# Transformer block: moving the hand-over from the key projection to the row maxima, and the loads around it

## The chip, the cores and the metric

The kernel runs on one core of one Trainium2 chip. The engines that do its work are TensorE (PE, with its weight loads shown apart as PEld), VectorE (DVE), ScalarE (ACT) and GpSimd (POOL). SyncE (SP) only issues transfers to the DMA engines, one after the other; its rows in a profile (SPq) show the issue, not the transfer. The metric is device time in microseconds (us), the median of several runs, lower is better. Before the change it is 1687.12 us, the median of three runs (1686.07 to 1687.93).

## The reference

One block with attention and an MLP, both scaled and shifted by a conditioning vector. S = 2048 positions, D = 512, 32 heads of 16, F = 1792, all in float32:

```python
mod = (_silu(c) @ w_mod).reshape(c.shape[0], 6, 1, -1)
sa, ca, ga, sb, cb, gb = (mod[:, i] for i in range(6))
h = _layernorm(x) * (1 + ca) + sa
qkv = h @ wqkv                                   # q, k, v: 32 heads of 16
p = softmax((q @ k.T) * 16 ** -0.5)              # full, 2048 x 2048 in each head
x = x + ga * ((p @ v) @ wo)
h = _layernorm(x) * (1 + cb) + sb
a = h @ w1 + b1
x = x + gb * ((a * tanh(softplus(a))) @ w2)
```

## The kernel before, in words

**Numbers in two halves.** Most operands of the products are split into a high part that TensorE multiplies in one pass and a low part that holds the rest (`hi_copy`, `lo_sub`, lines 86 to 95: names end in `h` and `l`). A product is then the sum of three: high by high, high by low, low by high (`mm3`).

**Projections (first part, up to about 48 us).** The normalised input is transposed into `h_h` and `h_l`, four blocks of 512 positions (`tb` 0 to 3). The weights of q, k and v come in slices (`slice_load`, tile `wr`), split by `slice_split` (L88 on ACT makes `wh`, L95 on POOL makes `wl`). `qk_unit` multiplies one slice by one block: 128 rows, which are 8 heads. Its `fin` takes the product out of its PSUM bank, splits it (`qh`, `ql`) and stores it in DRAM in `qscr` or `kscr`, each of the 16 rows of a head threefold: 48 rows. `v_unit` does the same for v, collects four blocks of 128 positions in a tile `vq` and stores them in `vscr` (L306). In the first part only slice 0 of the keys (all four blocks), slice 0 of the queries (block 0) and a little of v are made.

**Pairs.** Heads are worked on four at a time (a group, `n`), two and two: pair 0 and 1 are group 0, pair 2 and 3 group 1. `load_pair(pp)` loads a pair's queries (`load_q`, L321, tile `qa`, 50 rows for each head) and keys (`load_k`, L330, tile `ka`, 48 rows of 2048, with two more rows that a memset has filled with ones). For pairs 0 and 1 the keys are loaded block by block. There are five `qa` and five `ka` tiles (`NR`).

**Maxima (steps -20 to -1).** Before a group's scores are taken through the exponential, the maximum of each query's scores must be known. `max_pair` makes the scores of 128 queries against 512 keys for two heads (L596 on PE, into two banks of the `ring` in PSUM) and DVE reduces them to a maximum (L598, `mx`). Thirty-two such products serve group 0, eight more begin group 1. `neg_max` (L611, DVE) ends the reduction of a group, `max_rows` transposes the result (L617 on PE), ACT and DVE split its negative (`mh`, `mt`), and four small DMAs (L626, here called the rows of maxima) put it in rows 48 and 49 of the queries, where the ones in the keys add it to each score. The ring has four banks free for these products, two pairs, so PE can be two products ahead of DVE. Between two products PE does dense work: units of the projections still to do (`dense_slots`, `lanes`; L133).

**Main part (steps 0 to 511).** Each step makes scores (L637), takes their exponential on ACT (L640), multiplies an earlier step's by v (L655, tile `vg`, loaded by `load_v`, L569), makes products for the maxima of the next group (L582, reduced by L584) and, beside it, dense work: projections, then the output projection and the MLP. Weights of the MLP are split and put in DRAM ahead of time; the first six that way during the maxima (`early_load` and `early_prep`, tile `ep`, stored by L1595).

**What sets the order.** It is written out by hand. Each step `t` has two hook numbers, `h` = 2t and 2t + 1, and `at(h, f)` puts the work `f` at such a point. Nothing reorders it: each engine, and SP's queue, runs its instructions in that order, and each instruction waits for its own operands and buffers. A hook number therefore is a place in the order of each engine and no time. The maxima stage begins at `h` = -40, the scores at 0.

Of the kernel before, what the change touches and what calls it, by code (L numbers as in the profile page):

```python
# [8 lines left out]
F32 = mybir.dt.float32  # L9
# [9 lines left out]
def adaln_block(ctx: ExitStack, tc: tile.TileContext, x, wqkv, wo, w1, b1, w2, c, w_mod, out):  # L19
    nc = tc.nc  # L20
# [8 lines left out]
    NB = S // TB  # L29
# [53 lines left out]
    def dap(t, off, ap):  # L83
        return bass.AP(tensor=t.tensor, offset=t.offset + off, ap=ap)

    def hi_copy(eng, hi, src):
        if eng == "a":
            nc.scalar.copy(hi, src)  # L88
        elif eng == "v":
            nc.vector.tensor_copy(hi, src)  # L90
        else:
            nc.gpsimd.tensor_scalar(hi, src, 1.0, 0.0, op0=ALU.mult, op1=ALU.add)

    def lo_sub(eng, lo, src, hi):
        (nc.gpsimd if eng == "p" else nc.vector).tensor_sub(lo, src, hi.bitcast(F32))  # L95
# [15 lines left out]
    def mm3(acc, ah, al, bh, bl, late="a"):  # L111

        n = len(ah)
        seq = ((ah, bh), (ah, bl), (al, bh)) if late == "a" else ((ah, bh), (al, bh), (ah, bl))
        seq = [(l[k], r[k]) for l, r in seq for k in range(n)]
        for i, (l, r) in enumerate(seq):
            mm(acc, l, r, i == 0, i == len(seq) - 1)
# [21 lines left out]
    def pe_run():  # L139
        while pe_queue:  # L140
            mm_go(pe_queue.pop(0))
# [18 lines left out]
    def bank(tag="ms"):  # L160
        if not isinstance(tag, str):
            return tag
        return ring() if tag == "ring" else ps.tile([P, TB], F32, tag=tag, name="bk", bufs=1)
# [26 lines left out]
    def clear(h):  # L190

        return h if h < 60 or h % 32 < 25 else h - h % 32 + 34
# [10 lines left out]
    def at(h, f):  # L203

        hooks.setdefault(h, []).append(f)
# [4 lines left out]
    ka = [kq.tile([P, S], F32R, name=f"ka{i}") for i in range(2)]  # L210
# [25 lines left out]
    def slice_split(kind, i, pool=None, eng="p", hi_eng="a"):  # L236
        raw = slices[kind, i]
        w = raw.shape[2]
        hi = (pool or qp).tile([P, DK, w], F32R, tag="wh", name="wh", bufs=2)
        lo = (pool or qp).tile([P, DK, w], F32R, tag="wl", name="wl", bufs=2)  # L240
        hi_copy(hi_eng, hi, raw)
        lo_sub(eng, lo, raw, hi)
        slices[kind, i] = (hi, lo)

    def qk_unit(kind, ct, tb, tag):

        wh, wl = slices[kind, ct]
        acc = bank(tag)
        ts_ = slice(tb * TB, (tb + 1) * TB)
        mm3(acc, [wh[:, k, :] for k in range(DK)], [wl[:, k, :] for k in range(DK)],  # L250
            [h_h[:, k, ts_] for k in range(DK)], [h_l[:, k, ts_] for k in range(DK)], "b")

        def fin(h=None):
            late = h is not None and -4 <= h < 3
            if late and not spares:
                for v in range(2):
                    both = ap.tile([P, DK, TB], F32R, tag=f"o_{v}", name="late", bufs=1)
                    spares.extend(both[:, i, :] for i in range(DK))
            if late:
                qh, ql = spares.pop(), spares.pop()  # L260
            else:
                qh = qp.tile([P, TB], F32R, tag="qh", name="qh", bufs=2)
                ql = qp.tile([P, TB], F32R, tag="ql", name="ql", bufs=2)
            if h is None:
                hi_copy("a", qh, acc)
                lo_sub("v", ql, acc, qh)
            else:
                qf = (ap.tile([P, TB], F32, tag=f"p{len(spares) // 2 % 2 * 2}", name="qf", bufs=3) if late else
                      pw.tile([P, TB], F32, tag="raw", name="qf", bufs=1))
                nc.scalar.copy(qf, acc)  # L270
                hi_copy("p", qh, qf)
                lo_sub("p", ql, qf, qh)
            scr, rows = (qscr, 50) if kind == 0 else (kscr, 48)

            def put():
                put_away.add((kind, ct, tb))
                o = 8 * ct * rows * S + tb * TB
                if kind == 0:
                    for r, src in enumerate((qh, qh, ql)):
                        nc.sync.dma_start(dap(scr, o + r * S, [[rows * S, 8], [3 * S, DH], [1, TB]]), src.bitcast(F32))  # L280
                    return
                hi = qh.bitcast(F32)
                twice = bass.AP(tensor=hi.tensor, offset=hi.offset, ap=[list(hi.ap)[0], [0, 2], [1, TB]])
                nc.sync.dma_start(dap(scr, o, [[3 * S, P], [2 * S, 2], [1, TB]]), twice)
                nc.sync.dma_start(dap(scr, o + S, [[3 * S, P], [1, TB]]), ql.bitcast(F32))

            put() if h is None else at(clear(h + (5 if h > 60 else 2)), put)
        return fin
# [25 lines left out]
    def load_q(pp, rows=50):  # L314
        n, j = divmod(pp, 2)
        qb, g = divmod(n, G)
        h = 4 * g + 2 * j
        qt = qa[pp % NR].bitcast(F32)
        assert (0, h // 8, qb) in put_away, (pp, put_away)
        for s in range(2):  # L320
            nc.sync.dma_start(qt[64 * s:64 * s + rows, :], qscr[h + s, :rows, qb * TB:(qb + 1) * TB])  # L321
# [10 lines left out]
    def load_pair(pp):  # L332
        load_q(pp)
        load_k(pp)


    with ExitStack() as es:
# [65 lines left out]
        def apply_tb(tb):  # L403
            rs = rss.pop(tb)
            for i in range(4):
                xt = xts[4 * tb + i]
                nc.scalar.activation(xt, xt, AF.Identity, scale=rs[:, 1, i:i + 1], bias=rs[:, 2, i:i + 1])
# [110 lines left out]
        def unit(fin):  # L518
            pe_run()
            fin()  # L520

        constants()
        for tb in range(NB):
            if tb + 2 < NB:
                stats_tb(tb + 2)
            parts = []
            early = []
            for kind in (1, 0) if tb == 0 else (1,):
                fin = qk_unit(kind, 0, tb, "ring" if tb + 1 < NB else "ms")
                parts.append((pe_queue[2 * DK:], fin))  # L530
                early.append(pe_queue[:2 * DK])
                pe_queue.clear()
            if tb == 0:
                (kw, qw) = early
                early = [[m for k in range(DK) for m in (kw[k], qw[k], kw[DK + k])], qw[DK:]]
            pe_queue.extend(m for e in early for m in e)
            pe_run()
            if tb in (1, 2):
                for kc in (2 * tb - 2, 2 * tb - 1):
                    unit(v_unit(0, kc, "ring"))  # L540
            if tb + 1 < NB:
                tr_tb(tb + 1, CUT1)
            for late, fin in parts:
                pe_queue.extend(late)
                unit(fin)
            if tb + 1 < NB:
                tr_tb(tb + 1, CUT2)
            if tb + 2 < NB:
                apply_tb(tb + 2)
            if tb == 0:  # L550
                for pp in range(2):
                    load_q(pp, 48)
            for pp in range(2):
                if tb < 2:
                    load_k(pp, tb)
        slice_split(0, 1)


    kq2 = ctx.enter_context(tc.tile_pool(name="kq2", bufs=1))
    ka += [kq2.tile([P, S], F32R, name=f"ka{i}") for i in range(2, NR)]  # L560
    for t in ka[2:]:
        nc.gpsimd.memset(t.bitcast(F32), 1.0)
    ap = ctx.enter_context(tc.tile_pool(name="ap", bufs=1, reuse_waits="tile"))
    vgs = {}

    def load_v(n):
        assert {(2, n % G // 4, i) for i in range(NKC)} <= put_away
        t = ap.tile([P, VROW], F32, tag="vg", name="vg", bufs=2)
        nc.sync.dma_start(t, vscr[n % G])  # L569
        vgs[n] = t  # L570
# [1014 lines left out]
    def early_prep(i, h):  # L1585

        def split():
            scr, raw, hi, lo = raws[i]
            hi_copy("p", hi, raw)
            lo_sub("p", lo, raw, hi)  # L1590

        def put():
            scr, _, hi, lo = raws.pop(i)
            for v, part in enumerate((hi, lo)):
                nc.sync.dma_start(scr[:, v, :], part.bitcast(F32))  # L1595

        at(h, split)
        at(h + 3, put)

    for i in range(EARLY):  # L1600
        early_prep(i, (-38, -36, -34, -32, -27, -25)[i])

    def start_preps(h, i=EARLY, turn=0, puts=()):

# [15 lines left out]
    for n in range(NIT):  # L1620
# [3 lines left out]
            at(32 * (n - 1), lambda n=n: load_pair(2 * n + 1))  # L1624
        if n > 0:
            at(32 * n - 11, lambda n=n: load_v(n))
    at(-7, lambda: load_v(0))
    at(17, lambda: load_pair(4))
    for qb in range(NB - 1):
        t0 = 32 * G * (qb + 1) + 16  # L1630
# [3 lines left out]
    at(2 * (T - 28), lambda: load_ys((0, 1)))  # L1634
    at(2 * (T - 12), lambda: load_ys((2,)))
    at(2 * T - 30, tail_loads)
    for pp, h in ((2, -22), (3, -10)):
        at(h, lambda pp=pp: load_pair(pp))
    def run_hooks(h):
        for f in hooks.pop(h, []):  # L1640
# [6 lines left out]
    t = T + 2  # L1647
# [32 lines left out]
```

## Time and profile before

| what | value |
|---|---|
| median of three runs | 1687.12 us (1686.07 to 1687.93) |
| profiled execution, its own time | 1687.18 us |
| span from its first to its last instruction | 1685.4 us |
| PE, DVE, ACT, POOL busy | 99%, 85%, 81%, 48% of the span |
| DMA, mean over the span | 142 GB/s |

A row of the order of time reads: start, length, engine, line, operation, output and inputs, number of instructions joined in the row (x) and, in brackets, how long the engine had stood idle before it and what ended that. Rows of instructions of one kind next to each other are joined. A row of waits reads: who waited, for whom, total in us, times, longest. Matmuls overlap, so that the start of the next tells more than the length of one. A wait for several things is put down to the one that came last.

### The profile page before, as it was taken

How to read it: one execution, taken by the hardware profiler on the slowest of the kernel's cores; microseconds unless marked ns; L12 is line 12 of the kernel's file. 1: busy time of each engine (PE TensorE's matmuls, PEld its weight loads, DVE VectorE, ACT ScalarE, POOL GpSimd, SP SyncE). 2: the span in 40 equal slices, each digit the busy share in tenths (PEclk: the TensorE clock that was granted, in tenths of full speed). 3: DMA queues.
4: the chain of work that ended last, by engine and by line, in shares of the span. 5: the costliest groups of instructions: out<-in, count | busy, mean ns of one | idle time of the engine just before them, and what ended most of it. 6: DMA issues, size and time to landing. Idle time of an engine off the chain costs nothing.

```text
span 1685.4 us, 34363 instructions
## 1 busy us (share of the span) xinstructions
PE 1664.2 (99%) x12707; PEld 928.9 (55%) x12707; DVE 1431.5 (85%) x2372; ACT 1357.4 (81%) x2618; POOL 812.5 (48%) x839
## 2 busy tenths in 40 slices
PE   8999999999999999999999999999999999999998
PEld 6856655555445555555555455555555455555687
DVE  6988888888999988888889888888889888883377
ACT  7257777777778988888878998888878998889674
POOL 5655224755323664546323664556323664555442
PEclk9999999999999999999999999999999999999999
DMA  7886656777746334434255434534354433434261
GB/s 248 280 261 183 157 145 208 195 223 217 242 118 168 90 94 106 123 77 132 81 135 162 107 77 103 134 86 120 97 137 122 124 94 88 145 96 134 77 227 62
DMA packets 114984, 239.02 MB, mean 142 GB/s; under 512 B 24500, under 2 KB 50120, under 8 KB 108864
## 3 DMA queue, kind: packets, MB, share of 16 engines
q1 hardware_dynamic: 114808, 236.82, 49.8%
q8 instruction: 100, 1.64, 0.4%
q14 instruction: 68, 0.56, 0.1%
q10 hardware_dynamic: 8, 0.00, 0.0%
HBM read 180.48 MB, written 51.45 MB: 138 GB/s over the span
## 4 chain that ended last, share of the span: by engine, by line
PE 90%; DVE 4%; DMA 2%; ACT 2%; issue 1%; SPq 0%; POOL 0%; ACTq 0%; DVEq 0%; POOLq 0%
PE bk L655 29%; PE ring L637 22%; PE ring L582 19%; PE bk L133 12%; PE ring L1268 2%; PE ring L126 2%; DVE mx L598 1%; ACT pr L640 1%; PE bk L126 1%; DVE mx L584 1%; DMA ka<-kscr 1%; DMA wr<-in_A_wqkv 1%; DMA xt<-in_A_x 0%; PE ring L133 0%; PE ring L971 0%
## 5 line engine op out<-in xcount | busy, mean ns | idle before, releaser
L584 DVE TENSOR_REDUCE mx<-ring 128x1 f32<-128x512 f32 x1968 | 1222.4, 682 | 151.3 <-PE ring L582 134.5
L640 ACT ACTIVATE pr<-ring 128x512 f32<-128x512 f32 x2048 | 1078.2, 603 | 207.7 <-PE bk L133 112.8
L582 PE MATMUL ring<-ka,qa 64*128 64x512 f32 x1968 | 818.2, 429 | 1.4 <-ACT pr L640 1.2
L637 PE MATMUL ring<-qa,ka 64*128 64x512 f32 x2048 | 759.1, 402 | 3.3 <-ACT pr L640 1.9
L655 PE MATMUL bk<-pr,vg 128*32 128x512 f32 x4096 | 545.0, 604 | 0.0
L582 PEld LDWEIGHTS ring<-ka,qa 64*128 64x128 f32 x1968 | 350.5, 184 | 326.0 <-DVE mx L584 251.5
L637 PEld LDWEIGHTS ring<-qa,ka 64*128 64x128 f32 x2048 | 373.6, 184 | 191.4 <-DVE mx L584 113.3
L133 PE MATMUL bk<-h,w 64*128 64x512 f32 (+1 forms) x1080 | 278.0, 390 | 0.0
L133 PE MATMUL bk<-w,a_h 64*128 64x512 f32 x632 | 210.8, 413 | 0.0
L133 PEld LDWEIGHTS bk<-h,w 64*128 64x128 f32 x1080 | 178.4, 184 | 8.9 <-ACT pr L640 1.5
L655 PEld LDWEIGHTS bk<-pr,vg 128*32 128x32 f32 x4096 | 81.1, 108 | 135.8 <-issue 126.5
L133 PE MATMUL bk<-w,a_l 64*128 64x512 f32 x316 | 124.0, 393 | 0.0
L133 PEld LDWEIGHTS bk<-w,a_h 64*128 64x128 f32 x632 | 106.7, 184 | 3.2 <-ACT hb L849 0.8
L1027 POOL TENSOR_TENSOR y<-yd,y 128x512 f32<-128x512 f32 x44 | 56.8, 1292 | 88.9 <-ACT yd L1026 79.5
L861 POOL TENSOR_SCALAR qq<-ee 128x512 f32<-128x512 f32 x25 | 15.5, 621 | 169.4 <-ACT ee L855 169.4
L877 POOL TENSOR_TENSOR qq<-qq,rr 128x512 f32<-128x512 f32 x42 | 54.1, 1289 | 86.0 <-ACT rr L871 86.0
L863 POOL TENSOR_TENSOR hb<-hb,ee 128x512 f32<-128x512 f32 x42 | 54.1, 1289 | 79.7 <-DVE ee L859 77.7
L133 PE MATMUL bk<-w,o_hl 64*128 64x512 f32 x288 | 79.3, 405 | 0.0
L95 POOL TENSOR_TENSOR a_l<-hb,a_h 128x512 fp32r<-128x512 f32 x53 | 73.0, 1378 | 4.4
L133 PE MATMUL bk<-h_h,wl 64*128 64x512 f32 x192 | 62.0, 416 | 0.3 <-ACT pr L640 0.3
L133 PEld LDWEIGHTS bk<-w,a_l 64*128 64x128 f32 x316 | 58.3, 184 | 2.8
L879 POOL TENSOR_TENSOR rr<-rr,qq 128x512 f32<-128x512 f32 x42 | 54.1, 1289 | 3.5
(234 smaller groups left out, 1889.6 us busy)
## 6 DMA issues: line engine op xcount, KB each, us to landing
ka<-kscr SPq DMA_DIRECT2D x124, 384.0 KB
w<-w2scr SPq DMA_DIRECT2D x56, 512.0 KB
w<-w1scr SPq DMA_DIRECT2D x46, 512.0 KB
vg<-vscr SPq DMA_DIRECT2D x32, 552.0 KB
qa<-qscr SPq DMA_DIRECT2D x124, 100.0 KB
qscr<-qh SPq DMA_DIRECT2D x32, 256.0 KB
w2scr<-hl SPq DMA_DIRECT2D x14, 512.0 KB
kscr<-qh SPq DMA_DIRECT2D x12, 512.0 KB
```

The source lines that it names most:

```text
L95: (nc.gpsimd if eng == "p" else nc.vector).tensor_sub(lo, src, hi.bitcast(F32))
L126: nc.tensor.matmul(acc, l, r, start=start, stop=stop)
L133: i = nc.tensor.matmul(acc, l[64 * g:64 * g + 64], r[64 * g:64 * g + 64], start=start and not then, stop=bool(stop and then))
L582: nc.tensor.matmul(pm, qt[64 * s:64 * s + 64, qs * P:(qs + 1) * P], kt[64 * s:64 * s + 64, kb * TB:(kb + 1) * TB], start=True, stop=True)
L584: nc.vector.tensor_reduce(out=mxs[n][:, s, 4 * j + qs, kb:kb + 1], in_=pm, op=ALU.max, axis=AX.X)
L637: nc.tensor.matmul(p_, kt[64 * s:64 * s + 64, kc * P:(kc + 1) * P], qt[64 * s:64 * s + 64, :], start=True, stop=True)
L640: e = nc.scalar.activation(pr, p_, AF.Exp, scale=SCALE)
L655: nc.tensor.matmul(accs[n][32 * h:32 * h + 32, :], vgs[n][:, o:o + 32], pts.pop((t, h)), start=(kc == 0), stop=(kc == 15))
L863: (nc.vector if tail else nc.gpsimd).tensor_mul(hb, hb, ee)
L877: nc.gpsimd.tensor_mul(qq, qq, rr)
L879: nc.gpsimd.tensor_mul(rr, rr, qq)
L1027: nc.gpsimd.tensor_add(y[i], yd, y[i])
```

## The change

Six places of the order move; what is computed stays the same.

1. The last block of the keys in the first part (`kind` 1, `tb` 3) leaves its bank as later units do: ACT copies it to a tile `qf`, POOL makes both halves from that. Before, ACT made the high half and DVE the low half out of PSUM.
2. `slice_split(0, 1)`, which splits the next slice of the query weights, stands before that last block and no longer behind it.
3. The memsets of the key tiles 2 and 3 go behind POOL's two new operations, that of key tile 4 to `h` = -18.
4. The early weight preparations 3, 4 and 5 move from `h` = -32, -27, -25 to -27, -25, -23.
5. The load of pair 2 (the third pair) moves from `h` = -22 to -36, ahead of the stores of the early weights.
6. The load of the first values moves from `h` = -7 to -3 and that of pair 3 (the fourth) from -10 to -2, both behind the rows of maxima, which are sent at -6.

```diff
@@ -261,7 +261,7 @@
-            if h is None:
+            if h is None and (kind, tb) != (1, NB - 1):
                 hi_copy("a", qh, acc)
                 lo_sub("v", ql, acc, qh)
             else:
@@ -547,19 +547,19 @@
             if tb + 2 < NB:
                 apply_tb(tb + 2)
+            elif tb + 1 < NB:
+                slice_split(0, 1)
...
-        slice_split(0, 1)
-
...
-    for t in ka[2:]:
-        nc.gpsimd.memset(t.bitcast(F32), 1.0)
+    for i, h in ((2, -39), (3, -39), (4, -18)):
+        at(h, lambda t=ka[i]: nc.gpsimd.memset(t.bitcast(F32), 1.0))
@@ -1598,7 +1598,7 @@
-        early_prep(i, (-38, -36, -34, -32, -27, -25)[i])
+        early_prep(i, (-38, -36, -34, -27, -25, -23)[i])
@@ -1624,7 +1624,7 @@
-    at(-7, lambda: load_v(0))
+    at(-3, lambda: load_v(0))
@@ -1634,7 +1634,7 @@
-    for pp, h in ((2, -22), (3, -10)):
+    for pp, h in ((2, -36), (3, -2)):
         at(h, lambda pp=pp: load_pair(pp))
```

On DVE, at the end of the projections, the last subtraction goes and the first reduction follows the work on the transposed input:

```order
 L474 SCALAR_TENSOR_TENSOR hf<-bk,modc,h_h 128x512
 L477 TENSOR_SCALAR h_l<-hf,modc 128x512
-L95 TENSOR_TENSOR ql<-bk,qh 128x512
 L598 TENSOR_REDUCE mx<-ring 128x2 x32
 L611 TENSOR_REDUCE mm<-mx 128x4x4 x2
```

`ql<-bk,qh` is the low half of the last key block; it is now on POOL, behind a copy on ACT, where the split of the weights (`wh<-wr`) now comes first:

```order
 L473 ACTIVATE h_h<-ring,modc 128x512
 L473 ACTIVATE h_h<-bk,modc 128x512
-L88 CAST qh<-bk 128x512
 L88 CAST wh<-wr 128x512
+L270 COPY qf<-bk 128x512
 L601 COPY seen<-ring 128x2 x2
```

On SP's queue, at the beginning of the maxima, the queries and keys of pair 2 (`qa_102`, and `ka_695`, which is key tile 2) stood behind all stores of early weights and now stand ahead of the first of them:

```order
 L330 DMA ka_99<-kscr 48x512 x2
 L1582 DMA ep<-in_B_w 128x4x128 x2
-L1595 DMA w1scr<-ep 128x512 x8
+L321 DMA qa_102<-qscr 50x512 x2
+L330 DMA ka_695<-kscr 48x2048 x2
+L1595 DMA w1scr<-ep 128x512 x6
 L233 DMA wr<-in_A_wqkv 128x4x128
```

Two of the eight stores that stood there come later. At the end of the maxima SP's queue was, before, from the loads of pair 2 to the first of the rows of maxima (`qa_100<-mt`):

```order
L321 DMA qa_102<-qscr 50x512 x2
L330 DMA ka_693<-kscr 48x2048 x2
L306 DMA vscr<-vq 128x4x272 x2
L321 DMA qa_103<-qscr 50x512 x2
L330 DMA ka_694<-kscr 48x2048 x2
L284 DMA kscr<-qh 128x2x512
L285 DMA kscr<-ql 128x512
L569 DMA vg<-vscr 128x1104
L626 DMA qa_100<-mt 2x4x128
```

and is now, from the stores of values to the next modulation weights:

```order
L306 DMA vscr<-vq 128x4x272 x2
L284 DMA kscr<-qh 128x2x512
L285 DMA kscr<-ql 128x512
L626 DMA qa_100<-mt 2x4x128
L626 DMA qa_101<-mt 2x4x128
L626 DMA qa_100<-mt 2x4x128
L626 DMA qa_101<-mt 2x4x128
L233 DMA wr<-in_A_wqkv 128x4x128
L569 DMA vg<-vscr 128x1104
L321 DMA qa_103<-qscr 50x512 x2
L330 DMA ka_696<-kscr 48x2048 x2
L749 DMA wm<-in_w_mod 128x4x256 x2
```

The loads of pair 3 (`qa_103`) and of the first values (`vg`) have gone from ahead of the rows of maxima to behind them and behind one slice of weights.

## Prediction

> **What bounds the kernel now.** I read the page first, then busy time by stage, then the order of time on VectorE, TensorE, ScalarE and the DMA queue in the one stage that the change touches. On the page the last number of a row is a count.
>
> ```profile
> span 1685.4 us, 34363 instructions
> PE 1664.2 (99%) x12707; PEld 928.9 (55%) x12707; DVE 1431.5 (85%) x2372; ACT 1357.4 (81%) x2618; POOL 812.5 (48%) x839
> ```
>
> The view of stages says where that 99% isn't true (columns: stretch, then busy us of PE, PEld, DVE, ACT, POOL, granted clock, DMA share, GB/s).
>
> ```profile
> 48.00:84.00 36.00, 35.27 (x434) 33.41 (x434) 36.00 (x33) 6.51 (x21) 24.15 (x22) 1.00 0.93 293
> 84.00:98.00 14.00, 10.42 (x81) 7.94 (x83) 10.58 (x12) 2.54 (x7) 3.48 (x4) 1.00 1.00 290
> 98.00:112.00 14.00, 13.40 (x100) 7.27 (x98) 12.39 (x21) 11.44 (x23) 12.16 (x12) 1.00 1.00 364
> 112.00:1640.00 1528.00, 1522.76 (x11645) 815.69 (x11642) 1303.53 (x2191) 1281.42 (x2489) 734.32 (x737) 1.00 0.49 134
> ```
>
> From 112 us on PE is busy for 1522.76 of 1528.00 us, so that stretch is a block that moves as a whole when its start moves. From 48 to 84 the bound is DVE, busy for 36.00 of 36.00: it reduces the score products to row maxima. From 84 to 98 PE and DVE both stand for 3.5 us, with the DMA engines at share 1.00. The granted clock is 1.00 throughout, so nothing here is the throttle. The order of time on DVE shows the maxima stage whole (start, length, idle before and what ended it):
>
> ```profile
> 47.67 0.69 DVE L95 TENSOR_TENSOR ql<-bk,qh 128x512 fp32r<-128x512 f32 x1 [1.26 <-ACT qh L88]
> 48.28 36.34 DVE L598 TENSOR_REDUCE mx<-ring 128x2 f32<-128x1024 f32 x32
> 84.65 0.34 DVE L611 TENSOR_REDUCE mm<-mx 128x16 f32<-128x64 f32 x2
> 87.50 2.36 DVE L598 TENSOR_REDUCE mx<-ring 128x2 f32<-128x1024 f32 x2 [2.50 <-PE ring L596]
> 90.45 7.02 DVE L598 TENSOR_REDUCE mx<-ring 128x2 f32<-128x1024 f32 x6 [0.35 <-PE ring L596]
> ```
>
> The 32 reductions of pairs 0 and 1 run without a gap, 36.34/32 = 1.14 us apart. Their start is set by a subtraction of the last key block (47.67), their continuation by a hole of 2.50. On PE the same points:
>
> ```profile
> 46.90 0.49 PE L596 MATMUL ring<-ka,qa 64*128 64x512 f32 x2
> 48.21 0.50 PE L133 MATMUL ring<-h_h,wh 64*128 64x512 f32 x1 [0.81 <-ACT wh L88]
> 86.04 0.46 PE L596 MATMUL ring<-ka,qa 64*128 64x512 f32 x1 [2.40 <-DMA ka<-kscr]
> 86.99 0.47 PE L596 MATMUL ring<-ka,qa 64*128 64x512 f32 x1 [0.48 <-DMA ka<-kscr]
> 97.52 0.50 PE L637 MATMUL ring<-qa,ka 64*128 64x512 f32 x1 [0.43 <-DVE mx L598]
> ```
>
> The first product was in PSUM at 47.39, and DVE came to it at 48.28. The hole is a load: keys of pair 2, 2.40 and 0.48 us. The first score (L637, 97.52) waits for the last reduction, so DVE's end at 97.47 is what starts the long block.
>
> **The change, part by part.** *Last key block off DVE.* The high part's copy and DVE's subtraction become one ScalarE copy to SBUF and two POOL operations. DVE then waits for the first product alone. As 86.99 + 0.47 = 87.46 was followed by DVE at 87.50, I take 47.39 + 0.04 = 47.43, and the start moves by 0.85. The slice's split, moved ahead of that copy, has these rows:
>
> ```profile
> 45.09 1.04 POOL L479 TENSOR_TENSOR h_l<-hf,modc 128x512 fp32r<-128x512 f32 x1 [1.62 <-DVE hf L474]
> 47.05 0.59 ACT L88 CAST qh<-bk 128x512 fp32r<-128x512 f32 x1 [2.97 <-PE bk L126]
> 47.54 0.62 ACT L88 CAST wh<-wr 128x512 fp32r<-128x512 f32 x1
> 48.23 1.28 POOL L95 TENSOR_TENSOR wl<-wr,wh 128x512 fp32r<-128x512 f32 x1 [2.10 <-ACT wh L88]
> 64.64 0.62 POOL L92 TENSOR_SCALAR ep<-ep 128x512 fp32r<-128x512 f32 x1
> 66.60 1.29 POOL L95 TENSOR_TENSOR wl<-wr,wh 128x512 fp32r<-128x512 f32 x1
> 78.65 0.62 ACT L88 CAST wh<-wr 128x512 fp32r<-128x512 f32 x1
> ```
>
> ACT had idled 2.97 before 47.05, so `wh` fits there and is ready before 46; PE's dense products, which stood 0.81 for it, follow the first product at once, and `wl` can run from 46.13 to 47.41. The new copy waits for `wl` (same buffer), so it ends at about 48.0, and POOL's two operations by 50.0 (0.62 + 1.29, the lengths at 64.64 and 66.60). Nobody is near them: what they feed, the fourth key block, enters at the 25th product, 24 × 1.14 = 27 us later. Since PE's second and third products came late too, DVE gains between 0.85 and 0.95; I take 0.9. PE must then be 0.9 earlier with all that it reads. The tightest is the low half of the next slice, `wl` at 66.60 to 67.89. Moving the fourth weight preparation behind it lets it start at 64.64, where that preparation began, 2.0 sooner, which pays for the 0.9. The memsets only change places on POOL, busy for 24.15 of 36.00 here: cost 0 while its gaps cover them.
>
> *Third pair loaded earlier.* Its loads and the rows behind them stand on the DMA queue so (SPq is the issue, not the transfer; the last five are waits: total, count, longest):
>
> ```profile
> 61.18 0.94 SPq L1582 DMA_DIRECT2D ep<-in_B_w  x2
> 68.00 0.63 SPq L233 DMA_DIRECT2D wr<-in_A_wqkv  x1
> 77.44 1.59 SPq L321 DMA_DIRECT2D qa<-qscr  x2
> 79.12 0.77 SPq L330 DMA_DIRECT2D ka<-kscr  x2
> 80.98 2.57 SPq L321 DMA_DIRECT2D qa<-qscr  x2
> 90.16 0.33 SPq L569 DMA_DIRECT2D vg<-vscr  x1
> 90.59 3.02 SPq L626 DMA_DIRECT2D qa<-mt  x4
> 94.61 0.40 SPq L233 DMA_DIRECT2D wr<-in_A_wqkv  x1
> 95.53 1.00 SPq L749 DMA_DIRECT2D wm<-in_w_mod  x2
> 97.71 0.37 SPq L284 DMA_DIRECT2D kscr<-late  x1
> ...
> SPq L569 <- DMA vscr<-vq: 2.8, 2, 1.5
> SPq L284 <- DMA vg<-vscr: 1.1, 1, 1.1
> SPq L233 <- DMA ka<-kscr: 1.0, 1, 1.0
> SPq L749 <- DMA kscr<-ql: 0.2, 1, 0.2
> SPq L626 <- DMA ka<-kscr: 0.3, 1, 0.3
> ```
>
> The loads go from 77.44 to right behind 61.18 + 0.94. They took from 77.44 to 86.99, 9.6 us; started at 62.2 the same gives 71.8, and the products of pair 2 come at 86.04 − 2.40 − 0.9 = 82.7. So the hole goes wholly: 2.50, or 2.58 if the next reduction overlaps what is ahead of it as the others do (two in 2.36 at 1.14 apart make one 1.22 long, an overlap of 0.08). Before the stores of the first weights it pushes four issues ahead: those stores, the next slice and the values' stores come up to about 4.5 us later. The slice was issued at 68.0 and first used by ACT at 78.65. That leaves 10.6 us for a load; 10.6 − 0.9 − 4.5 still leaves 5.2. This is one of two thin covers.
>
> *Fourth pair and first values behind the rows of maxima.* The rows (L626) complete the queries, so no score can start without them. The fourth pair's transfers (issued from 80.98) end when L233 is let go, 94.61; the stores ahead of them had landed at 90.16, where L569 stopped waiting: 4.45 us on full DMA engines. `vg` landed by 97.71, the key stores ahead of it between 95.53 and 96.53, where the second L749 waited for them: some 1.5. The first of the rows were there when L637 started, so for them 97.5 is the latest. Without 4.45 + 1.5 ahead of them they land at about 91.6; the other end is 97.5. I take 91.6, since L626 itself waited for `ka<-kscr`: it stood behind that load. They are needed at 97.52 − 3.45 = 94.1, so 2.5 us are left: the second thin cover.
>
> [...]
>
> Behind the rows, values and pair 3 have these first readers, 3.45 earlier then:
>
> ```profile
> 104.57 1.06 PE L655 MATMUL bk<-pr,vg 128*32 128x512 f32 x8
> 108.48 0.72 PE L582 MATMUL ring<-ka,qa 64*128 64x512 f32 x2
> ```
>
> From 91.6, a slice (at most 1.0: it was issued at 94.61), `vg` (1.5) and the pair (4.45) land by about 94.1 and 98.6; needed at 101.1 and 105.0.
>
> The sum: 0.9 + 2.55 = 3.45. The profiled execution took 1687.18 (span 1685.4), 0.06 above the median of the runs, 1687.12. 1687.18 − 3.45 = **1683.7**, 0.2% below the median. A measurement of this kernel tells about 0.2%, 3.4 us, from no change, so the forecast stands right on that bound.
>
> **Rivals.**
>
> *The first gain is lost.* DVE or PE starts early and stands later for a slice or for POOL, which gets 0.62 + 1.29 more work. Against: both covers above. Then only 2.55 is won: 1684.6. A form of it with its own chance: POOL's new subtraction (1.29) holds up the reduction beside it for its whole length. Then 3.45 − 1.29 = 2.2 is won, time 1685.0; against it, POOL was busy 24.15 us of the 36.00 in which DVE showed no gap. [...]
>
> *The change doesn't do what it says: the rows come late.* If the DMA engines have no less ahead of the rows, they land up to 97.5, and all but 0 to 2.5 is taken back: 1685 to 1687.2, say 1686.0. For: share 0.93 and 1.00, and bytes moved earlier delay what follows. Against: 6 us of transfers really leave the front.
>
> *Slower.* Pair 3 is issued after the rows, from about 91, with value and weight loads beside it. If PE stands at L582 for it (108.48 in this profile), time is lost from the point where pair 3 lands after 108.5. For: before, it needed 13.6 us from its first issue (80.98) to 94.61. Against: 91 + 13.6 = 104.6 is still before 105.0. It needs 17.5 us to end level; at 21 us, 1690.7.
>
> *More.* From 98 to 112 PE stands another 0.60 (13.40 of 14.00) with DMA at 1.00. If the lighter queue frees that too: 1683.1.
>
> **How the numbers follow.** Both gains and no new wait: 0.69, at 1683.7, own range 1682.9 to 1684.5. More: 0.11. First gain lost: 0.07, 0.02 of it by the shared port. Rows late: 0.06. Slower: 0.07. The 0.2% bound is at 1683.75; the main case lies a shade beyond it, and runs scatter by 0.9 to either side (1686.07 to 1687.93), so 0.41 of its 0.69 count as faster and 0.28 as the same. With More, faster is 0.52; with the two part losses and 0.01 of the slower case, same is 0.42; slower is 0.06. The range goes from More with half the scatter, 1682.5, to the middle of late rows, 1685.7.
>
> **What would show it.** Right: no `ql` by DVE at 47.67, the first reduction near 47.4 and the 32nd ending near 83.7; no wait of L596 for `ka<-kscr`; the first L637 near 94.1, let go by DVE; PE from then as full as before. Wrong: L637 let go by `qa<-mt` (rows late), L582 by `ka<-kscr` near 105 (slower), a gap among the 32 reductions ended by POOL or ACT (first gain lost).

## The result and the profile after

The changed kernel takes **1682.73 us** (median of 22 runs, 1681.42 to 1684.93) against 1686.90 us for the kernel before on the same chip (22 runs, 1684.47 to 1688.87): a ratio of 0.9976, 95% interval 0.9970 to 0.9983. That is 4.2 us less, with 2.9 to 5.1 us as its interval. A second measurement, below, gives 3.6 us. The two profiled executions lie 1687.18 − 1683.78 = 3.40 us apart. The forecast was 3.45 and 1683.7.

The page of the profile after, its first part (span, then busy time, share and count of each engine):

```profile
span 1682.0 us, 34366 instructions
PE 1663.0 (99%) x12707; PEld 928.8 (55%) x12707; DVE 1431.6 (85%) x2371; ACT 1357.6 (81%) x2618; POOL 815.0 (48%) x841
```

DVE has one instruction less and POOL two more, with 2.5 us more to do. The view of stages of the kernel after (busy us of PE, PEld, DVE, ACT, POOL, then the clock granted to PE as a share of its full speed, DMA share, GB/s):

```profile
48.00:80.50 32.50, 32.33 (x411) 30.99 (x409) 32.50 (x30) 6.36 (x20) 23.77 (x23) 1.00 1.00 296
80.50:94.00 13.50, 12.04 (x97) 8.99 (x94) 12.83 (x14) 2.23 (x7) 4.18 (x5) 1.00 0.80 272
94.00:108.00 14.00, 13.35 (x98) 7.42 (x98) 12.30 (x20) 11.75 (x24) 11.82 (x12) 1.00 1.03 308
108.00:1636.00 1528.00, 1522.23 (x11644) 816.18 (x11641) 1303.93 (x2191) 1281.09 (x2488) 734.34 (x737) 1.00 0.49 135
```

The end of the maxima stage, where PE and DVE had each stood for 3.5 of 14 us, now has DVE busy for 12.83 of 13.50. The long block of 1528 us is as full as it was (1522.23 us of PE against 1522.76), so what was won was won ahead of it. The order of time on DVE, kernel after:

```profile
47.17 36.30 DVE L598 TENSOR_REDUCE mx<-ring 128x2 f32<-128x1024 f32 x32 [1.05 <-PE ring L596]
83.50 0.35 DVE L611 TENSOR_REDUCE mm<-mx 128x16 f32<-128x64 f32 x2
83.76 2.35 DVE L598 TENSOR_REDUCE mx<-ring 128x2 f32<-128x1024 f32 x2
86.71 7.02 DVE L598 TENSOR_REDUCE mx<-ring 128x2 f32<-128x1024 f32 x6 [0.36 <-PE ring L596]
94.35 7.33 DVE L584 TENSOR_REDUCE mx<-ring 128x1 f32<-128x512 f32 x12 [0.63 <-PE ring L582]
```

The subtraction of the key block is gone from DVE, the first reduction waits for PE's first product alone, and the hole of 2.50 us ahead of pair 2's reductions is gone. On PE, kernel after, from the first product of the maxima to the first loads' readers of the main part:

```profile
46.60 0.50 PE L596 MATMUL ring<-ka,qa 64*128 64x512 f32 x2
46.94 0.39 PE L133 MATMUL ring<-h_h,wh 64*128 64x512 f32 x1
93.78 0.50 PE L637 MATMUL ring<-qa,ka 64*128 64x512 f32 x1 [0.43 <-DVE mx L598]
100.89 1.07 PE L655 MATMUL bk<-pr,vg 128*32 128x512 f32 x8
104.80 0.72 PE L582 MATMUL ring<-ka,qa 64*128 64x512 f32 x2
```

Before, the first product started at 46.90 and the first score at 97.52, 50.62 us apart. Now it is 46.60 and 93.78, 47.18 apart: 3.44 us less. The first score is let go by DVE, and neither the values (L655) nor pair 3 (L582) make PE wait. The rest of the way, from the first score to the end of the span, is 1587.9 us before and 1588.2 after. (The first product came 0.30 earlier; in the profiles below it starts anywhere from 45.79 to 47.44.) That span of 47.18 us, **first product to first score**, is the measure in the experiments.

### The profile page after: what moved, and what is told of

Read it like the earlier page. It is cut to its first block, busy times and chain, and to the rows that moved or that the text cites. A ratio compares the mean times of both kernels' runs of the same rounds, so it can differ in the third digit from the quotient of the medians.

```text
span 1682.0 us, 34366 instructions
## 1 busy us (share of the span) xinstructions
PE 1663.0 (99%) x12707; PEld 928.8 (55%) x12707; DVE 1431.6 (85%) x2371; ACT 1357.6 (81%) x2618; POOL 815.0 (48%) x841
## 4 chain that ended last, share of the span: by engine, by line
PE 89%; DVE 5%; ACT 2%; DMA 2%; issue 1%; SPq 0%; POOL 0%; ACTq 0%; DVEq 0%; POOLq 0%
PE bk L655 29%; PE ring L637 21%; PE ring L582 19%; PE bk L133 11%; DVE mx L598 2%; PE ring L1268 2%; DVE mx L584 2%; PE ring L126 2%; ACT pr L640 1%; PE bk L126 1%; DMA ka<-kscr 1%; PE ring L133 1%; DMA wr<-in_A_wqkv 0%; PE ring L971 0%; PE ring L617 0%
## 5 line engine op out<-in xcount | busy, mean ns | idle before, releaser
L582 PE MATMUL ring<-ka,qa 64*128 64x512 f32 x1968 | 818.0, 429 | 2.3 <-ACT pr L640 1.1
L655 PE MATMUL bk<-pr,vg 128*32 128x512 f32 x4096 | 545.1, 604 | 0.0
L582 PEld LDWEIGHTS ring<-ka,qa 64*128 64x128 f32 x1968 | 350.6, 184 | 327.1 <-DVE mx L584 252.7
L655 PEld LDWEIGHTS bk<-pr,vg 128*32 128x32 f32 x4096 | 81.2, 108 | 135.6 <-issue 126.4
```

The costliest lines, as they stand in the source:

```text
L582: nc.tensor.matmul(pm, qt[64 * s:64 * s + 64, qs * P:(qs + 1) * P], kt[64 * s:64 * s + 64, kb * TB:(kb + 1) * TB], start=True, stop=True)
L655: nc.tensor.matmul(accs[n][32 * h:32 * h + 32, :], vgs[n][:, o:o + 32], pts.pop((t, h)), start=(kc == 0), stop=(kc == 15))
```

## The experiments

Each profile is one execution. The places are the six of the change. "Score" is when the first score starts, "way" is the time from first product to first score, in us; the times are medians, and each ratio is to runs of the kernel before taken beside them. For the experiments those were taken in three sets, with medians of 1686.61, 1687.08 and 1686.60, the last two on another chip than the first, so a difference of two medians of this table can hold some tenths of a microsecond that the kernels did not make.

| places made | first product | score | way | median | ratio |
|---|---|---|---|---|---|
| none (before) | 46.90 | 97.52 | 50.62 | 1686.90 | |
| 1 to 4 | 47.44 | 96.62 | 49.18 | 1687.28 | 1.0001 (0.9992 to 1.0010) |
| 5 | 46.18 | 94.21 | 48.03 | 1684.03 | 0.9987 (0.9977 to 0.9996) |
| 6 | 46.20 | 98.00 | 51.80 | 1687.10, one run | |
| 5 and 6 | 45.79 | 93.82 | 48.03 | 1683.72 | 0.9985 (0.9976 to 0.9995) |
| 1 to 5 | 47.06 | 95.60 | 48.54 | 1688.13 | 1.0003 (0.9994 to 1.0013) |
| 2 to 6 | 46.76 | 94.74 | 47.98 | 1684.42 | 0.9984 (0.9974 to 0.9993) |
| all but 4 | 45.79 | 93.61 | 47.82 | 1684.14, one run | |
| all, pair 3 ahead of the rows | 46.56 | 94.11 | 47.55 | 1684.17 | 0.9985 (0.9975 to 0.9995) |
| all, values ahead of the rows | 45.81 | 93.00 | 47.19 | 1682.55 | 0.9978 (0.9968 to 0.9988) |
| all (after) | 46.60 | 93.78 | 47.18 | 1682.73 | 0.9976 (0.9970 to 0.9983) |
| all, again | 47.31 | 94.48 | 47.17 | 1683.05 | 0.9981 (0.9972 to 0.9990) |

**Hand-over alone (places 1 to 4).** Against the changed kernel:

```diff
-    at(-3, lambda: load_v(0))
+    at(-7, lambda: load_v(0))
-    for pp, h in ((2, -36), (3, -2)):
+    for pp, h in ((2, -22), (3, -10)):
```

> The changed kernel with its three moved loads put back (pair 2 at -22, pair 3 at -10, values at -7); the new hand-over, memsets and order of preparations stay. Measured inside the trace: from the start of the first product L596 to the start of the first score L637, 50.62 us before (46.90 to 97.52), 47.18 with the whole change. Theory (the keys of pair 2 land when the DMA queue lets them, whatever DVE does): the first reduction follows the first product in 0.6 us, but the hole at product 33 grows from 2.5 to 3.4 us; 50.5 us, and a time 0 to 0.4 us under the kernel before. Rival (the two gains add, each by itself): hole 2.5 us, 49.7 us, time 0.9 us under it.

The way is 49.18 us, 1.44 less and more than either theory expected. The time did not move. The profile shows both halves of that. On PE:

```profile
84.35 0.47 PE L596 MATMUL ring<-ka,qa 64*128 64x512 f32 x1 [0.64 <-DMA ka<-kscr]
96.62 0.46 PE L637 MATMUL ring<-qa,ka 64*128 64x512 f32 x1 [2.16 <-DMA qa<-mt]
```

The hole for pair 2's keys is 0.64 instead of 2.40 and 0.48. By the order of SP's queue place 4 does that: two of the stores of early weights now come behind pair 2's loads, whose issue starts at 75.54 instead of 77.44. Neither theory had counted that, and no run shows it apart from the other places. The first product also came 0.54 later than in the profile of before, which shortens such a hole too. But now the first score waits 2.16 us for the rows of maxima. And this wait has a sequel, in the view of busy time by stretch of the same run:

```profile
94.73:98.14 3.41, 1.52 (x14) 1.31 (x14) 1.07 (x3) 1.91 (x5) 3.33 (x4) 1.00 0.93 292
98.14:104.97 6.83, 6.69 (x27) 4.26 (x25) 5.32 (x9) 4.58 (x10) 2.16 (x3) 0.50 1.06 396
```

After a stretch in which PE was busy for 1.52 of 3.41 us, the granted clock is 0.50 for 6.83 us, in the part where PE is the bound.

**Third pair alone (place 5).** Against the kernel before:

```diff
-    for pp, h in ((2, -22), (3, -10)):
+    for pp, h in ((2, -36), (3, -10)):
```

> The kernel before with pair 2 loaded at -36 in place of -22, all else as before; pair 3 and the first values stay ahead of the rows of maxima. Theory (the rows of maxima wait behind those loads, and set the first score once the hole is gone): no wait of L596 for keys, but L637 let go by the rows at about 95.9; 49.0 us from first product to first score, time about 1.6 us under the kernel before. Rival (the rows are there early enough anyway): 48.1 us, 2.5 us under it.

The rival was right: 2.59 us of the way and 2.6 us of the time.

```profile
46.18 0.50 PE L596 MATMUL ring<-ka,qa 64*128 64x512 f32 x2
94.21 0.50 PE L637 MATMUL ring<-qa,ka 64*128 64x512 f32 x1 [0.43 <-DVE mx L598]
```

The first score is let go by DVE. My theory had the rows late here, and they were not: pair 2's loads no longer stand ahead of them either, and the second of the four rows landed at 93.81 instead of 97.34. The second is the one that counts, since the first step works with the heads whose rows are sent first. In the four runs whose first score waits for rows (places 1 to 4 alone, and three below) it starts 0.13 to 0.14 us after that landing. In the kernel before that makes 97.48, and the score, let go by DVE, started at 97.52: the rows there were as good as the bound already.

**Both loads (places 5 and 6).** Against the kernel before:

```diff
-    at(-7, lambda: load_v(0))
+    at(-3, lambda: load_v(0))
-    for pp, h in ((2, -22), (3, -10)):
+    for pp, h in ((2, -36), (3, -2)):
```

> The kernel before with all three loads moved as in the change, and nothing else: hand-over, memsets and preparations as before. Theory (two separate holes): 48.1 us from first product to first score, L637 let go by DVE, time 2.5 us under the kernel before. Rival (the hand-over is the larger part, the hole would only turn up elsewhere): 49.7 us or more, at most 0.9 us under it.

As expected, 48.03. With place 5 alone it was 48.03 too: behind the old hand-over, place 6 is worth nothing. What places 1 to 4 add to this is 48.03 − 47.18 = 0.85 us, the hand-over's gain with all loads out of its way.

**All but place 6.** Against the changed kernel:

```diff
-    at(-3, lambda: load_v(0))
+    at(-7, lambda: load_v(0))
-    for pp, h in ((2, -36), (3, -2)):
+    for pp, h in ((2, -36), (3, -10)):
```

> The changed kernel with pair 3 put back to -10 and the first values to -7, so both stand ahead of the rows of maxima again. Theory (rows behind 1.5 MB of loads set the first score): DVE done at the same time as with the whole change, then L637 waits for the rows; 49.0 us from first product to first score, the same as with the third pair alone, so that the earlier hand-over brings nothing here; time about 1.6 us under the kernel before. Rival (the place of these loads does not matter): 47.2 us, 3.4 us under it.

The way is 48.54, 1.36 more than after the change and nearer to my theory's 49.0 than to 47.2. The time is not near it: the median is 5.4 us above that after the change (4.6 by the ratios), and the whole gain is gone. Its PE and DMA queue rows, and the view by stretch:

```profile
95.60 0.46 PE L637 MATMUL ring<-qa,ka 64*128 64x512 f32 x1 [1.79 <-DMA qa<-mt]
```

```profile
88.92 0.33 SPq L569 DMA_DIRECT2D vg<-vscr  x1
89.35 2.79 SPq L626 DMA_DIRECT2D qa<-mt  x4
```

```profile
93.44:96.85 3.41, 1.62 (x15) 1.08 (x12) 1.45 (x3) 1.82 (x4) 3.25 (x4) 1.00 0.84 263
96.85:103.68 6.83, 6.54 (x27) 4.25 (x27) 5.08 (x9) 4.60 (x9) 2.31 (x4) 0.50 1.03 383
```

The rows are issued at 89.35, 2.9 us later than after the change (86.41), since the loads of pair 3 and of the values are issued in front of them and the values' load stands 1.3 us on SP for its stores. Then the first score waits 1.79 us, and from 96.85 the clock is at one half for 6.83 us. In this kernel 8 of 10 runs have a granted clock of 0.998 or less over their whole length, and the same is true of places 1 to 4 alone, whose score also waits for the rows. Of the changed kernel's 33 runs it is 3. (Of the kernel before it is 9 of 31, 22 of 30 and 10 of 21 in its three sets, so the count differs between sets of one kernel too.) A spell of 6.83 us at one half takes 0.002 off the mean clock of such a run. PE has 27 products in this one and 29 in the 3.41 us behind it, so my estimate is that it costs up to half its length, 3.4 us.

**The same wait with PE busy in it.** Place 6 undone as in the last run, and products that nobody reads put into the wait (the lines that undo place 6 left out):

```diff
                 ring_of[0] = NRING
+                for _ in range(6):
+                    nc.tensor.matmul(ring_t[:, ring_at[0] % NRING, :], ka[0][64:, :P], ka[0][64:, :TB], start=True, stop=True)
```

> The changed kernel without its place 6, as before, and six extra 64x512 products of keys by keys on TensorE just ahead of the first score, into the PSUM bank that the first score overwrites (nothing reads them). They run while the rows of maxima are still on their way, so the wait stays and TensorE is not idle in it. Theory (clock): the wait costs 1.36 us by itself (first product to first score 48.5 us, as without the filler), and the rest of what the loads ahead of the rows cost was the granted clock at one half after the idle hole of 1.79 us. Then the hole is under 0.7 us, the granted clock is 1.00 from 96 to 106 us, from first score to end 1587.3 to 1588.3 us, and the median is near 1682.7 + 1.4 = 1684.1 us. Rival (the transfers behind the rows, or the later work itself, cost the rest): the median stays near 1688.1 us, with the clock as low or with other waits between 96 and 110 us.

```profile
94.22 1.19 PE L1418 MATMUL ring<-ka 64*128 64x512 f32 x4 [0.43 <-DVE mx L598]
95.71 0.39 PE L637 MATMUL ring<-qa,ka 64*128 64x512 f32 x1
```

```profile
94.45:97.86 3.41, 3.41 (x21) 2.22 (x20) 1.70 (x3) 2.22 (x6) 3.24 (x5) 1.00 0.90 275
97.86:104.69 6.83, 6.33 (x46) 3.81 (x47) 6.16 (x11) 5.25 (x11) 4.07 (x3) 1.00 1.06 399
```

L1418 is the filler. The rows are late again, though 0.5 us less: the second lands 47.86 us after the first product, against 48.40 without the filler. The first score now follows the filler's end, so that the way, 48.67 us, is no shorter than without it, and the clock stays at 1.00. The median is 1684.82 us (ratio 0.9988, 0.9979 to 0.9997) against 1688.13 without the filler: products that nobody reads made the kernel some 3 us faster (3.3 by the medians, 2.5 by the ratios), and 2 of 10 runs are at 0.998 or less instead of 8. The kernel before was at 0.998 or less more often beside this run (22 of 30) than beside the one without the filler (9 of 31), so the set doesn't explain that. The two intervals overlap at their ends (0.9994 to 0.9997), so the size is rough, but the theory's 1684.1 and the rival's 1688.1 are told apart. Of what place 6 saves, 1.4 us is the wait and some 3 the clock after it. The single profiles tell the size no better: from first score to end they take 1589.4 and 1589.6 us with the spell (this kernel without the filler, and places 1 to 4 alone), 1585.7 with the filler, where 1587.3 to 1588.3 was expected, and 1586.4 to 1588.7 in the other eleven.

**Pair 3 ahead of the rows, and the values ahead of the rows.** Each against the changed kernel:

```diff
-    for pp, h in ((2, -36), (3, -2)):
+    for pp, h in ((2, -36), (3, -10)):
```

> The changed kernel with the load of the fourth pair back ahead of the rows of maxima, the first values still behind. Theory (the rows wait for all that was issued ahead of them): the rows land 4.45 us later than at 90.3 us, so at 93 to 94.8 us; the first score comes 0 to 1.0 us later (first product to first score 47.2 to 48.2 us), TensorE's idle before it is 0.4 to 1.4 us; median 1682.7 to 1684 us. Rival (the values, not the pair, made the rows late in the run with both ahead): 47.2 us, no loss, rows near 91 us.

```diff
-    at(-3, lambda: load_v(0))
+    at(-7, lambda: load_v(0))
```

> The changed kernel with the load of the first values back ahead of the rows of maxima, the fourth pair still behind. Theory (thin cover of 2.5 to 3.5 us): the values' issue waits for their stores and takes 1.5 us to land, the rows land 1.5 to 3 us later, at 91.8 to 93.3 us, still before the last reduction (93.7 us): first product to first score 47.2 us, median as after the change, 1682.7 us, within 0.5. Rival: the queue stands behind the values' wait longer than that and the rows land after 93.8 us: 47.3 to 48.3 us, median up to 1684 us and more where the clock falls.

With pair 3 ahead (DMA queue, then PE):

```profile
86.38 2.78 SPq L626 DMA_DIRECT2D qa<-mt  x4
```

```profile
94.11 0.47 PE L637 MATMUL ring<-qa,ka 64*128 64x512 f32 x1 [0.80 <-DMA qa<-mt]
```

With the values ahead (PE):

```profile
93.00 0.50 PE L637 MATMUL ring<-qa,ka 64*128 64x512 f32 x1 [0.43 <-DVE mx L598]
```

The first is a clean measure of the queue: the rows are issued at the same time as after the change (86.38 and 86.41), and the trace has the last of them landed at 94.4 instead of 90.3, 4.1 us later, near the 4.45 of my sum. The second of them, which lets the score go, lands at 93.97 instead of 89.00, 5.0 us later. After the change it had been some 4.6 us early (89.00 + 0.14, against the score at 93.78); that cover goes, and the way is 0.37 longer. The median is 1.4 us up, but the two ratios' intervals overlap (0.9975 to 0.9995 and 0.9970 to 0.9983). Five of the ten runs are at 0.998 or less, with a median of 1685.96 against 1683.17 for the other five, though this profile has no spell after the first score. The values alone change nothing (47.19 us, 1682.55): the last of the rows lands at 92.9, still ahead of DVE. So one load ahead of the rows costs little or nothing here; place 6 is needed where both stand there, and the values could stand on either side.

**The last block on DVE again (places 2 to 6).** Against the changed kernel:

```diff
-            if h is None and (kind, tb) != (1, NB - 1):
+            if h is None:
```

> The changed kernel without its place 1: the last key block is split by ScalarE and VectorE out of PSUM as before; places 2 to 6 stay. Theory (the hand-over's gain is this block's subtraction on VectorE): the first reduction starts about 0.85 us later after the first product, first product to first score 48.0 us as in the run with the loads alone (48.03), median 1683.6 us. Rival (the order of the weight split, the memsets and the preparations gave part of it): 47.4 to 47.8 us, median 1683.1 us.

```profile
47.53 0.69 DVE L95 TENSOR_TENSOR ql<-bk,qh 128x512 fp32r<-128x512 f32 x1 [1.25 <-ACT qh L88]
48.14 36.28 DVE L598 TENSOR_REDUCE mx<-ring 128x2 f32<-128x1024 f32 x32
```

The way is 47.98: without place 1, 0.80 of the hand-over's 0.85 goes. Places 2 to 4 by themselves bring 0.05 (48.03 − 47.98); 2 and 3 have no run of their own. The median is 1.7 us above that of the changed kernel, 0.8 more than expected.

**The preparations as before (all but place 4).** Against the changed kernel:

```diff
-        early_prep(i, (-38, -36, -34, -27, -25, -23)[i])
+        early_prep(i, (-38, -36, -34, -32, -27, -25)[i])
```

> The changed kernel with place 4 undone: the early preparations 3, 4 and 5 where they were. Theory (the preparation ahead of the slice's low half holds that back, and the cover of 2 us that place 4 gives is needed): TensorE stands 0.3 to 0.9 us near 65 to 68 us for the low half wl, first product to first score 47.4 to 47.9 us. Rival (TensorE, two products ahead of VectorE, has room for it): no wait that reaches VectorE, 47.2 us.

On PE and on DVE:

```profile
66.93 0.50 PE L133 MATMUL bk<-h_h,wl 64*128 64x512 f32 x1 [0.41 <-POOL wl L95]
```

```profile
68.41 14.88 DVE L598 TENSOR_REDUCE mx<-ring 128x2 f32<-128x1024 f32 x13 [0.47 <-PE ring L596]
```

The theory holds: PE stands 0.41 us for `wl`, the wait reaches DVE as 0.47, and the way is 47.82. Without place 4, 0.64 of the hand-over's gain goes again: place 1 makes that gain and place 4 keeps it, so the two shares do not add. This is one run.

**Place 6 alone.** Against the kernel before:

```diff
-    at(-7, lambda: load_v(0))
+    at(-3, lambda: load_v(0))
-    for pp, h in ((2, -22), (3, -10)):
+    for pp, h in ((2, -22), (3, -2)):
```

> The kernel before with place 6 alone: the fourth pair and the first values behind the rows of maxima. Theory: pair 2's hole of 2.4 to 2.6 us stays, VectorE's last reduction sets the first score as before: first product to first score 50.5 to 50.6 us, rows 4 to 6 us earlier than at 97.1 to 97.8 us; no gain that counts. Rival (the rows had been the bound before): more than 0.3 us less, under 50.3 us.

No gain, and the rival falls, though by little, as the rows of the kernel before had been only 0.04 us ahead of the bound. But the way is 51.80, longer than in either theory. PE, DVE, then the stretches around the hole:

```profile
85.40 0.47 PE L596 MATMUL ring<-ka,qa 64*128 64x512 f32 x1 [2.46 <-DMA ka<-kscr]
86.64 0.62 PE L596 MATMUL ring<-ka,qa 64*128 64x512 f32 x1 [0.77 <-DMA ka<-kscr]
```

```profile
87.29 1.23 DVE L598 TENSOR_REDUCE mx<-ring 128x2 f32<-128x1024 f32 x1 [3.00 <-PE ring L596]
89.07 1.23 DVE L598 TENSOR_REDUCE mx<-ring 128x2 f32<-128x1024 f32 x1 [0.55 <-PE ring L596]
```

```profile
83.38:86.79 3.41, 0.62 (x3) 0.37 (x5) 0.88 (x3) 0.16 (x1) 0.00 (x0) 1.00 1.04 311
86.79:90.20 3.41, 3.41 (x16) 2.55 (x15) 2.36 (x2) 0.00 (x0) 0.00 (x0) 0.50 0.96 334
```

The first product came 0.70 us earlier than in the profile of before (46.20), the products with pair 2's keys only 0.64 and 0.35 earlier (85.40 and 86.64 against 86.04 and 86.99). So the hole grew to 3.00 on DVE. That is 0.5 of the 1.2 us by which the way is longer; the other 0.7 lies behind it, in a spell of half clock in which DVE waits another 0.55 for PE. The hole of the kernel before thus has no fixed size: it is the lateness of a chain of transfers against a chain of reductions, and an early start of the products tends to lengthen it (3.00 us with the first product at 46.20, 2.50 at 46.90).

**The kernel before with its hole filled, and the changed kernel again.** Against the kernel before:

```diff
+        if (n, jq, kb) == (1, 0, 0):
+            for _ in range(8):
+                nc.tensor.matmul(pm[:, 0, :], ka[0][:64, :P], ka[0][:64, :TB], start=True, stop=True)
         for s in range(2):
```

> The kernel before, with eight extra 64x512 products of keys by keys on TensorE ahead of the first product of pair 2, into the bank that this product overwrites (nothing reads them). They lie in the hole of 2.40 us in which TensorE waits for pair 2's keys. Theory (clock): the hole itself stays (first product to first score 50.6 us, DVE's hole of 2.50 us as before) but TensorE's idle in it falls under 0.8 us; some executions of the kernel before paid for this hole with a spell of half clock, so with the filler the median is 0.3 to 1.0 us under that of the kernel before in the same call. Rival (the kernel before is not touched by the clock, only its wait counts): the same median within 0.3 us.

> The changed kernel once more, beside the kernel before and the one with the filler on the same chip. Both theories: 1682.7 us, first product to first score 47.2 us. Theory (clock): the gain against the filled kernel before is nearer to 3.4 us than the gain against the kernel before is. Rival: both gains are the same within 0.3 us.

In the filled kernel the lines behind the filler count three more. Its DVE at the hole, and its first score on PE:

```profile
86.49 2.36 DVE L601 TENSOR_REDUCE mx<-ring 128x2 f32<-128x1024 f32 x2 [0.95 <-PE ring L599]
96.88 0.46 PE L640 MATMUL ring<-qa,ka 64*128 64x512 f32 x1 [0.80 <-DMA qa<-mt]
```

In this execution the first product came late (47.44), the hole was only 0.95 us, and then the first score waited 0.80 us for the rows: with a small hole they are the bound of the kernel before. The way is 49.44, where 50.6 was expected. The median is 1687.15 us against 1686.60 (ratio 1.0008, 0.9996 to 1.0020): the gain of 0.3 to 1.0 us that the clock theory asked for is not there. Three of 11 runs are at a granted clock of 0.998 or less, against 10 of 21 of the kernel before beside them, too few to say that the filler kept the clock up. The rival's "same within 0.3 us" lies inside the interval, and the medians are 0.55 apart. Whether the clock costs the kernel before anything at this hole stays open: the stretch behind it is bound by DVE and leaves PE some room (in the profile of before DVE is busy for 3.06 and PE for 2.79 of the 3.41 us from 88.48 on), but in the profile with place 6 alone the spell there did reach DVE. The changed kernel gained 3.55 us this time (1.7 to 4.7), and 4.1 against the filled kernel, which neither theory had. The 3.55 agrees with 3.4, and the 4.2 of the first measurement has 3.4 inside its interval.

## Why the prediction was right

*Last key block off DVE: 0.85 to 0.95, taken as 0.9.* By the runs 0.85, of which 0.80 goes without place 1. In the rows, the first reduction starts 0.57 us after the first product instead of 1.38, which is 0.81. The low end of my range was the right one: the added 0.05 for PE's late second and third products was not there. The order around it came as worked out, on ACT and POOL of the kernel after:

```profile
43.66 0.62 ACT L88 CAST wh<-wr 128x512 fp32r<-128x512 f32 x1
47.30 0.59 ACT L270 COPY qf<-bk 128x512 f32<-128x512 f32 x1 [3.01 <-POOL wl L95]
```

```profile
45.79 1.47 POOL L95 TENSOR_TENSOR wl<-wr,wh 128x512 fp32r<-128x512 f32 x1
48.68 1.28 POOL L95 TENSOR_TENSOR ql<-qf,qh 128x512 fp32r<-128x512 f32 x1
63.33 1.28 POOL L95 TENSOR_TENSOR wl<-wr,wh 128x512 fp32r<-128x512 f32 x1
```

The split of the weights went into ACT's idle time, the copy ended at 47.89 (about 48.0), POOL at 49.96 (50.0). The next `wl` starts at 63.33 instead of 66.60, and the run without place 4 shows that this was needed: without it PE waits.

*Third pair loaded earlier: 2.50 to 2.58, taken as 2.55.* In two runs 2.59, with 2.6 and 2.9 us in the times. The slice's load, the first thin cover, held. What I did not see is that the hole is not fixed: on DVE 2.50 in the profile of before, 3.00 and 0.55 with place 6 alone, 0.95 with the filler. That the sum came out to 0.01 us is partly luck: it rests on one profile of the kernel before, which showed a middling hole.

*Fourth pair and first values behind the rows.* The rows were expected at 91.6 and needed at 94.1, a cover of 2.5. The last of them landed at 90.3 and the second, which the first score needs, at 89.0, with the score at 93.8, so the cover was about 4.6. DMA queue of the kernel after:

```profile
86.41 2.78 SPq L626 DMA_DIRECT2D qa<-mt  x4
89.67 0.50 SPq L569 DMA_DIRECT2D vg<-vscr  x1
91.00 0.78 SPq L330 DMA_DIRECT2D ka<-kscr  x2
```

The 4.45 us for pair 3 ahead of them measured 4.1 for the last row and 5.0 for the second. That run is what shows that the rows land behind what was issued ahead of them; the wait of L626 for keys, 0.3 us before the change, from which I took it that the rows stood behind that load, is only a wait of SP before the issue. The step had place 6 keep the gains of the others, and so it does; its price without it I put at 1686.0, when the rows are late. It was 1688.1, outside the 1685 to 1687.2 of that rival.

*The step that was incomplete* is "the granted clock is 1.00 throughout, so nothing here is the throttle". It was true of that profile and no reason to leave the clock out: a wait of 1.8 us at the first score is followed by 6.83 us at one half, and with products in that wait the median is some 3 us lower. None of my rivals had that. It did not decide here because the forecast's own case has no such wait.

*The range and the bound.* Two ends of the range are not what I said they were: 1683.1 less half the scatter is 1682.65, not 1682.5, and the middle of 1685 to 1687.2 is 1686.1, not 1685.7. Both medians of the changed kernel, 1682.73 and 1683.05, lie inside either way, near the low end. The forecast stood on the bound of 0.2%; the two measurements lie on either side of it, at 0.24% and 0.19%.

*The rivals.* "By the shared port" is the form in which POOL's subtraction holds up the reduction beside it. That subtraction, 1.28 us from 48.68 on, runs beside reductions that go on at 36.30/32 = 1.13 us each without a gap, against 36.34/32 = 1.14 before, so it falls. No run shows a port that the two engines share, and moving the block from DVE to POOL took 0.80 us off the way. More: PE stands 0.65 us between 94 and 108, as it stood 0.60; it did not come. Slower: L582 at 104.80 has no wait.

## What to carry to other kernels

A load that must be early and a small transfer that must be prompt do not belong on one queue in the wrong order: four transfers of 4 KB landed 4 to 5 us later with a pair of heads issued ahead of them. Repairs of one chain do not add up: the early pair alone gave 2.6 us, the hand-over alone and the rows' place alone nothing, and the three together 3.6 to 4.2, since each uncovers the next wait. Where PE is the bound, price a wait just ahead of it with the half clock that may follow (here 6.83 us at 0.50 behind a wait of 1.79), and look for it in more than one execution. Ask of a small transfer in parts which part the reader needs first: here it was the second of four.

## What was not expected of the hardware

The granted clock fell to 0.50 for 3.41 us or twice that after stretches of 3.41 us in which PE was about half idle or more. Three cases stand above: 1.52 and 1.62 us busy of 3.41 before 6.83 us at one half, and 0.62 before 3.41 us. In the second profile of the changed kernel it happened in the projections:

```profile
18.27:21.68 3.41, 1.62 (x8) 0.76 (x6) 3.34 (x6) 3.21 (x5) 2.41 (x6) 1.00 1.06 387
21.68:25.09 3.41, 3.03 (x11) 2.58 (x11) 3.34 (x7) 1.94 (x3) 1.00 (x1) 0.50 1.04 298
```

The spells seem to lie on a fixed grid, whatever waits lie between them: in the hand-over run one ends at 26.46 and others begin at 98.14 and 1685.34, which is 71.68 and then 1587.20 us, or 21 and 465 steps of 3.4133 us. With place 6 alone they begin at 15.11 and at 86.79, again 71.68 apart, with the waits of 2.46 and 0.77 us in between. Counted back in such steps from the spell that ends the profile of before (0.50 from 1685.92, just behind the end of the span), its hole of 2.40 us falls across two stretches, and no spell followed:

```profile
81.66:85.07 3.41, 1.99 (x18) 1.42 (x14) 3.30 (x5) 0.16 (x1) 0.95 (x1) 1.00 0.91 181
85.07:88.48 3.41, 1.95 (x14) 1.66 (x16) 0.98 (x1) 0.00 (x0) 0.00 (x0) 1.00 1.08 347
```

So a wait of 1.79 us was followed by the half clock and one of 2.40 was not. The point is not sharp: in the run with place 6 alone a stretch with 1.91 us busy, from 11.70 to 15.11, was followed by a spell, and in the profile of before one with 1.85 us, from 20.22 to 23.63, was not. So the busy time of a stretch, as the trace has it, does not settle it alone. As to where the two waits lie, the one of 1.79 us, from 93.81 to 95.60, fell into one stretch whole, and the one of 2.40, from 83.64 to 86.04, into two, with 1.43 and 0.97 us.

What stays open is the exact condition, and how much of the scatter between runs of one kernel, some 3 us, it makes. Runs at 0.998 or less are the longer ones in most kernels: three such with the third pair alone have a median of 1687.34 us, the other seven 1683.81, and in the three sets of the kernel before the difference is 0.8 to 1.8. But with the values ahead of the rows it is the other way (1682.14 for two, 1683.33 for seven), and from first score to end the profiles without a spell there differ by 1585.7 to 1588.7 us, which no run explains.
